# Two waits and three evictions in the preparation of a recurrent layer's chunks

## The chip, the cores and the metric

The kernel runs on one core of one Trainium2 chip. The metric is the device time of one execution in microseconds (us). A core has five engines with a queue each, which run beside one another and wait for one another by semaphores: PE (TensorE: matmuls and transposes into PSUM), DVE (VectorE), ACT (ScalarE), POOL (GpSimd) and SP (SyncE, which issues most DMAs). An engine takes its instructions in the order in which the program lists them, so one that waits holds all that stand behind it on its engine.

## The reference

A recurrence over 768 steps, for 4 batches of 8 heads with a 40x40 state each, gives the tokens of a mixture of experts:

```
for t in range(768):                     # 32 states of 40 x 40
    y[t]  = r[t] @ state
    Sa    = state @ a[t]
    state = state * w[t] - outer(Sa, b[t]) + outer(v[t], k[t])
x = y as 3072 tokens of 320
for each token: e = argmax(x @ w_gate)   # one of 8 experts
    out = softmax gate * sigmoid gate * (relu(x @ w1[e]) @ w2[e])
```

## The kernel before, in words

The 768 steps are cut into 12 chunks of 64 (c = 0 to 11); the heads are treated in two halves (q = 0, 1). A chunk goes through these stages.

- **Scan** (`scan`, lines 104 to 124): w and D (that is a, k, b) are loaded; DVE forms running products P and I of the decays (line 116, 1.8 us each), rq (line 121) and I times rq (line 123). ACT's Square (line 119) writes over w with (w - 0.9) squared and sums it up; only a check of the input's range at the end reads the sum. Before the next chunk's w can be loaded, a small DVE memset (line 108) waits for that Square. The Square reads nothing but w, but since it overwrites w it can start only when both scans have read it.
- **Prep** (`prep`, from line 137): ACT squares rq into rs (line 181, a sum for the same check). Av is put together by POOL (lines 185, 184; by DVE for chunks 0 and 1) and a small ACT copy of P (line 187). From Av come Am (line 201 on ACT and 203 on POOL for chunk 2; DMAs for other late chunks) and rows of LA. DVE forms KBt (line 212). Then, for two sides with three groups each, PE multiplies KBt and Am into a PSUM tile pl (line 225), and pl is evicted: its upper half of N (line 234 on DVE for chunk 0, line 236 on ACT for every other chunk), its lower half of N (line 236, ACT), and LA (line 238, ACT). The tiles pl, and the tiles pt of the transposes behind them (line 163, copied out by ACT at line 165), share two PSUM buffers, so PE cannot write a group before ACT has evicted the one two back.
- **Inverse** (`tinv`, line 254): DVE forms the triangular inverse T from N, chunk 0 alone, chunk 1 alone, then two chunks at a time. It begins with a transpose that needs all of N (line 266 for chunks 0 and 1; line 271 for a pair) and ends with a transpose (line 330 or 336).
- **Crit** (`crit`, line 368): the recurrence proper, for c and q one after the other: PE applies LA, T and N (lines 379 and 392), ACT moves the results (As, line 383; XU, lines 422 and 423), and for chunks 0 and 1 DVE adds a correction in two instructions (line 405, the "As pair"). The next chunk's state is formed at lines 430 to 439.
- **Tail** (`tail`, line 444): PE and DVE form the outputs pY (lines 479 and 480) and x (line 482), and the router takes x.

Behind the twelve chunks the experts follow, on PE with little else.

The order of the instructions on each engine is made by a scheduler when the program is built, from the order of the code, the buffers that come free, and its own planned times. `issue_after(m)` adds a wait: the instructions inside are placed, and issued, behind the instruction m. `s.mark['n', c]` is the last eviction of N at line 236 for chunk c, as the code has it (the last lower half of the second side). The scheduler's choices at one place change what it finds free at the next, so a small edit can move many instructions.

Of the kernel before, what the change touches and what calls it, by code (L numbers as in the profile page):

```python
# [14 lines left out]
AF = mybir.ActivationFunctionType  # L15
# [34 lines left out]
def pat(x, off, dims):  # L50

    return bass.AP(x.tensor, x.offset + off, [x.ap[0]] + [list(d) for d in dims])


class Att:
# [47 lines left out]
    def scan(s, c):  # L103

        nc, V = s.nc, s.nc.vector
        n = 12 * 2 * 33
        w = s.p1.tile([120, n + 1], F32, name="w")
        V.memset(w[:, n:], 0.0)
        nc.sync.dma_start(out=w[:, 0:n], in_=s.win[c])
        s.D = s.p1.tile([120, 12, 3, C], F32, name="D")  # L110
        s.mark[c] = nc.sync.dma_start(out=s.D, in_=s.din[c]).ins
        P, I = (s.p1.tile([120, 12, 2, 33], F32, name=x) for x in "PI")
        Pf, If = (x.rearrange("p r h t -> p (r h t)") for x in (P, I))
        with s.tc.issue_after(s.mark['t', 0]) if c == 2 else ExitStack():
            for o, d in ((Pf, w[:, 0:n]), (If[:, ::-1], w[:, n:0:-1])):
                V.tensor_tensor_scan(out=o, data0=d, data1=s.rst, initial=0.0, op0=ALU.mult, op1=ALU.add)
        wq = pat(w, 1, [(33, 24), (1, 32)])
        with s.tc.issue_after(s.mark['n', 0]) if c == 1 else ExitStack():
            nc.scalar.activation(out=wq, in_=wq, func=AF.Square, bias=s.wb, accum_out=s.wsq[:, c:c + 1])
        rq = s.p1.tile([120, 24], F32, name="rq", bufs=2)  # L120
        V.reciprocal(out=rq, in_=P[:, :, :, 32])
        I3 = I.rearrange("p r h t -> p (r h) t")
        V.tensor_tensor(out=I3, in0=I3, in1=rq.unsqueeze(2).broadcast_to([120, 24, 33]), op=ALU.mult)
        s.Q = P, I, rq
# [12 lines left out]
    def prep(s, c):  # L137

        nc = s.nc
        g, V = nc.gpsimd, nc.vector  # L140
        st = s.st[c] = {}
        P, I, rq = s.Q
# [35 lines left out]
                nc.sync.dma_start(out=LA[0:40, :, 6 * j:6 * j + ng, :], in_=Ag[40 * j:40 * j + 40, :, 0:ng])  # L178

        rs = s.p1.tile([120, 24], F32, name="rs", bufs=2)  # L180
        nc.scalar.activation(out=rs, in_=rq, func=AF.Square, accum_out=s.rqm[:, c:c + 1])
        a, kb = D[:, :, 0], D[:, :, 1:3]
        with s.tc.issue_after(s.mark['r', 0]) if c == 1 else ExitStack():
            (g if c > 1 else V).tensor_tensor(out=Av[:, :, 0:33], in0=a[:, :, 0:33], in1=I[:, :, 1, ::-1], op=ALU.mult)
            (g if c > 1 else V).tensor_tensor(out=Av[:, :, 33:64], in0=a[:, :, 33:64], in1=P[:, :, 0, 1:32], op=ALU.mult)
        with s.tc.issue_after(s.mark['n', 0]) if c == 1 else ExitStack():
            nc.scalar.copy(out=Av[:, :, 64:66], in_=P[:, :, :, 32])
        Ag = Av.rearrange("p (a g) t -> p a g t", a=2)
        if c and c != 2:
            for j in range(3):  # L190
                r, n = slice(40 * j, 40 * j + 40), 6 if j < 2 else 4
# [26 lines left out]
        for side in range(2):  # L218
            Am = s.Am[:, side]
            yield  # L220
            for g0 in range(0, 6, 2):
                pl = s.ps.tile([128, 2, 3, C], F32, name="pl", tag="pl" if c or g0 == 0 else "tl", bufs=2 if c or g0 == 0 else 3)
                nj = 3 if g0 < 4 else 2
                for i in range(2):
                    nc.tensor.matmul(pl[:, i, 0:nj], KBt[:, 6 * side + g0 + i].rearrange("p n t -> p (n t)"), Am[:, g0 + i:g0 + i + 6 * nj - 5:6, 0:64],  # L225
                                     start=True, stop=True)
                pv = pl.rearrange("p g j t -> p j g t")
                for h in range(2):
                    r = slice(64 * side + 32 * h, 64 * side + 32 * h + 32)
                    n = C - 32 * h  # L230
                    nn = pat(N[r], C * g0, [(6 * C, nj), (C, 2), (1, n)])
                    pn = pv[64 + 32 * h:96 + 32 * h, 0:nj, :, C - n:]
                    if c == 0 and not h:
                        V.tensor_scalar(out=nn, in0=pn, scalar1=-1.0, scalar2=None, op0=ALU.mult)
                    else:
                        s.mark['n', c] = nc.scalar.activation(out=nn, in_=pn, func=AF.Copy, scale=-1.0).ins  # L236
                la = pat(LA[64:128, side], 66 * g0, [(396, nj), (66, 2), (1, 64)])
                nc.scalar.activation(out=la, in_=pv[0:64, 0:nj], func=AF.Copy, scale=-1.0)  # L238
                for i in range(2):
                    g.affine_select(out=la[:, :, i], in_=la[:, :, i], pattern=[[0, nj], [1, C]], base=0, channel_multiplier=-1,  # L240
                                    compare_op=ALU.is_gt, fill=0.0)
                yield
# [344 lines left out]
class Moe:  # L587
# [346 lines left out]
    def experts(s, ctx, verdict):  # L934
# [21 lines left out]
        def unit(e, t0, nt, prep):  # L956

            for _ in s.expert(nt, W[e], T[e, t0], lambda: s.hp, ps1, ps2) if (e, t0) != (0, 0) else s.E0:
                next(prep, None)
            for _ in prep:  # L960
                pass
# [199 lines left out]
```

## Time and profile before

| what | value |
|---|---|
| time, median of 3 runs | 682.52 us (681.66 to 682.61) |
| the profiled execution's own time | 678.98 us |
| its span, first to last instruction | 677.2 us |
| PE busy | 630.9 us (93%) |
| DVE busy | 464.9 us (69%) |
| ACT busy | 340.2 us (50%) |
| POOL busy | 233.8 us (35%) |
| mean granted TensorE clock | 0.97 of full |

The profiled execution is the one that the rows below describe. Its span is 1.8 us shorter than its own time, and that time is 3.5 us under the median of the timed runs; a difference worked out in the profile is carried over to the median. A granted clock of 1.00 is 2.4 GHz and one of 0.50 is 1.2 GHz. Busy shares are means over the stretches of a program that has very different ones: the chunks run until about 440 us, the experts after that.

### The profile page before, as it was taken

How to read it: one execution, taken by the hardware profiler on the slowest of the kernel's cores; microseconds unless marked ns; L12 is line 12 of the kernel's file. 1: busy time of each engine (PE TensorE's matmuls, PEld its weight loads, DVE VectorE, ACT ScalarE, POOL GpSimd, SP SyncE). 2: the span in 40 equal slices, each digit the busy share in tenths (PEclk: the TensorE clock that was granted, in tenths of full speed). 3: DMA queues.
4: the chain of work that ended last, by engine and by line, in shares of the span. 5: the costliest groups of instructions: out<-in, count | busy, mean ns of one | idle time of the engine just before them, and what ended most of it. 6: DMA issues, size and time to landing. Idle time of an engine off the chain costs nothing. (4 is left out here: it accounts for less than half of the span.)

```text
span 677.2 us, 21154 instructions
## 1 busy us (share of the span) xinstructions
PE 630.9 (93%) x8871; PEld 564.3 (83%) x8871; DVE 464.9 (69%) x911; ACT 340.2 (50%) x783; POOL 233.8 (35%) x337
## 2 busy tenths in 40 slices
PE   7787988898999999989999889899999999999996
PEld 6475877787988888878889779799999999999985
DVE  8868689969986997699399654374774545654231
ACT  2577762784378357637743354253573435343120
POOL 9655321341144258314204111335342333211112
PEclk9667999999999999999999979999999999999999
DMA  5995763276346726643224752263774344431001
GB/s 141 179 184 132 175 156 82 78 165 168 98 128 166 157 80 168 173 97 99 83 80 126 194 165 76 58 195 85 213 203 152 115 135 134 150 103 34 19 11 32
DMA packets 56305, 84.45 MB, mean 125 GB/s; under 512 B 26848, under 2 KB 43515, under 8 KB 54763
## 3 DMA queue, kind: packets, MB, share of 16 engines
q1 hardware_dynamic: 52331, 74.05, 42.3%
q0 software_dynamic: 3872, 8.97, 4.7%
q8 instruction: 72, 1.18, 0.7%
q14 instruction: 30, 0.25, 0.1%
HBM read 67.59 MB, written 8.96 MB: 113 GB/s over the span
## 5 line engine op out<-in xcount | busy, mean ns | idle before, releaser
L863 DVE SCALAR_TENSOR_TENSOR hl<-ph,hh 128x480 fp32r<-128x480 f32 (+1 forms) x74 | 41.3, 567 | 65.4 <-ACT hh L862 65.3
L862 ACT ACTIVATE hh<-ph 128x480 fp32r<-128x480 f32 (+1 forms) x74 | 36.7, 501 | 93.5 <-PE ph L858 93.1
L878 POOL DMA_INDIRECT out_dram<-y,ti x32 | 34.3, 1073 | 141.5 <-DVE y L877 80.8
L873 PE MATMUL po<-w2h,hh 128*120 128x320 f32 x256 | 78.3, 311 | 0.2 <-ACT hh L862 0.2
L874 PE MATMUL po<-w2l,hh 128*120 128x320 f32 x256 | 77.6, 309 | 0.0
L858 PE MATMUL ph<-xh,w1h 128*128 128x480 f32 (+1 forms) x222 | 76.1, 347 | 0.3 <-DVE mem L704 0.3
L858 PE MATMUL ph<-xl,w1h 128*128 128x480 f32 (+1 forms) x222 | 75.7, 344 | 0.0
L875 PE MATMUL po<-w2h,hl 128*120 128x320 f32 x256 | 74.9, 308 | 0.0
L225 PE MATMUL pl<-Am,KBt 120*128 120x192 f32 (+1 forms) x288 | 62.9, 352 | 7.7 <-ACT LA L238 6.2
L240 POOL TENSOR_SCALAR_AFFINE_SELECT LA<-LA 64x192 f32<-64x192 f32 x144 | 55.2, 418 | 40.2 <-ACT LA L238 38.8
L383 ACT ACTIVATE As<-pa,hq 128x320 f32<-128x320 f32 x80 | 42.1, 528 | 47.2 <-PE pa L392 36.0
L236 ACT ACTIVATE N<-pl 32x192 f32<-32x192 f32 (+1 forms) x138 | 51.6, 374 | 26.3 <-PE pa L392 12.2
L225 PEld LDWEIGHTS pl<-Am,KBt 120*128 120x128 f32 x288 | 47.1, 205 | 13.4 <-ACT LA L238 8.7
L480 PE MATMUL pY<-KB,M 128*64 128x64 f32 (+1 forms) x768 | 53.3, 225 | 3.0 <-DVE M L468 3.0
L479 PE MATMUL pY<-Sd,R 128*64 128x64 f32 (+1 forms) x704 | 53.9, 227 | 0.0
L392 PE MATMUL pa<-As,Tc 64*32 64x40 f32 x1792 | 51.1, 204 | 2.9 <-ACT As L383 2.1
L730 POOL DMA_INDIRECT tab<-rec,si x24 | 29.9, 1245 | 67.6 <-DMA tab<-rec,si 45.5
L464 PE MATMUL pM<-R,VU 128*128 128x128 f32 x384 | 52.3, 287 | 0.9 <-ACT VU L456 0.8
L480 PEld LDWEIGHTS pY<-KB,M 128*64 128x64 f32 x768 | 46.9, 138 | 6.6 <-DVE M L468 3.4
L838 POOL DMA_INDIRECT xg<-xd,ti x32 | 35.8, 1118 | 44.6 <-PE px L821 32.7
L392 PEld LDWEIGHTS pa<-As,Tc 64*32 64x32 f32 x1792 | 40.3, 112 | 12.8 <-issue 3.8
L858 PE MATMUL ph<-xh,w1l 128*128 128x480 f32 (+1 forms) x148 | 50.7, 344 | 0.0
(198 smaller groups left out, 1571.2 us busy)
## 6 DMA issues: line engine op xcount, KB each, us to landing
D<-in_din_dram SPq DMA_DIRECT2D x12, 1080.0 KB
st<-in_w_dram SPq DMA_DIRECT2D x16, 512.0 KB
st<-in_w_dram SPq DMA_DIRECT2D x16, 480.0 KB
XS<-in_vt_dram SPq DMA_DIRECT2D x24, 256.0 KB
XU<-in_vt_dram SPq DMA_DIRECT2D x24, 256.0 KB
VU<-in_vl_dram SPq DMA_DIRECT2D x24, 208.0 KB
w<-in_win_dram SPq DMA_DIRECT2D x12, 371.2 KB
st<-in_w_dram SPq DMA_DIRECT2D x16, 256.0 KB
```

The source lines that it names most:

```text
L225: nc.tensor.matmul(pl[:, i, 0:nj], KBt[:, 6 * side + g0 + i].rearrange("p n t -> p (n t)"), Am[:, g0 + i:g0 + i + 6 * nj - 5:6, 0:64], sta ...
L236: s.mark['n', c] = nc.scalar.activation(out=nn, in_=pn, func=AF.Copy, scale=-1.0).ins
L240: g.affine_select(out=la[:, :, i], in_=la[:, :, i], pattern=[[0, nj], [1, C]], base=0, channel_multiplier=-1, compare_op=ALU.is_gt, fill=0.0)
L383: s.mark['as'] = nc.scalar.activation(out=x, in_=pa, func=AF.Copy, scale=s.hq[:, h:h + 1]).ins
L392: nc.tensor.matmul(pa[o + w:o + w + 32, i], m(p)[o:o + 64], x[o:o + 64, i, :], start=start, stop=True, tile_position=(o, o + w), skip_grou ...
L464: nc.tensor.matmul(pM[:, i], VU[:, h0 + i].rearrange("p n t -> p (n t)"), R[:, :, h0 + i], start=True, stop=True)
L479: nc.tensor.matmul(o, R[:, side, i, :], Sf[:, 40 * i:40 * i + w], start=True, stop=False)
L480: s.mark['y'] = nc.tensor.matmul(o, Ms[i // 4][:, i % 4, side, :], Kf[:, k:k + w], start=not c, stop=True).ins
L858: nc.tensor.matmul(ph, l, r, start=(i == 0), stop=(i == 7))
L873: nc.tensor.matmul(po, hh[f][:, ts_], w2h[:, f], start=(f == 0), stop=False)
L874: nc.tensor.matmul(po, hh[f][:, ts_], w2l[:, f], start=False, stop=False)
L875: nc.tensor.matmul(po, hl[f][:, ts_], w2h[:, f], start=False, stop=(f == 7))
```

## The change

Three edits, all in the first chunks:

1. The Square of chunk 3 is held behind the last eviction of N of chunk 2 (that of chunk 1 was already held behind chunk 0's; that of chunk 2 stays free).
2. rs of chunk 2 is held behind the last eviction of N of chunk 1.
3. The upper halves of N of chunk 1's second side (three groups) are evicted by DVE at line 234 in place of ACT at line 236.

```
@@ scan
-        with s.tc.issue_after(s.mark['n', 0]) if c == 1 else ExitStack():
+        with s.tc.issue_after(s.mark['n', c - 1]) if c in (1, 3) else ExitStack():
             nc.scalar.activation(out=wq, in_=wq, func=AF.Square, bias=s.wb, accum_out=s.wsq[:, c:c + 1])
@@ prep
         rs = s.p1.tile([120, 24], F32, name="rs", bufs=2)
-        nc.scalar.activation(out=rs, in_=rq, func=AF.Square, accum_out=s.rqm[:, c:c + 1])
+        with s.tc.issue_after(s.mark['n', c - 1]) if c in (2,) else ExitStack():
+            nc.scalar.activation(out=rs, in_=rq, func=AF.Square, accum_out=s.rqm[:, c:c + 1])
...
-        with s.tc.issue_after(s.mark['n', 0]) if c == 1 else ExitStack():
+        with s.tc.issue_after(s.mark['n', c - 1]) if c in (1,) else ExitStack():
             nc.scalar.copy(out=Av[:, :, 64:66], in_=P[:, :, :, 32])
...
-                    if c == 0 and not h:
+                    if not h and (c == 0 or c == 1 and side >= 1):
                         V.tensor_scalar(out=nn, in0=pn, scalar1=-1.0, scalar2=None, op0=ALU.mult)
                     else:
                         s.mark['n', c] = nc.scalar.activation(out=nn, in_=pn, func=AF.Copy, scale=-1.0).ins
```

The third hunk of the diff writes the wait of the small copy into Av in another form and leaves it as it was. In the kernel after, lines from 182 on stand one line lower than before (236 is 237, and so on).

The two queues below are those on which the steps of the prediction rest. The first place is ACT at the second side of chunk 1. pl_440, pl_448 and pl_456 are the three groups of that side, N_225 is N of chunks 0 and 1, w_497 belongs to chunk 2, Am_127 and Av_567 are those of chunk 2. Before:

```order
L238 ACTIVATE LA_392<-pl_440 64x3x2x64
L119 ACTIVATE w_497,wsq_142<-w_497,wb_140 120x24x32
L383 ACTIVATE As_603<-pa_541,hq_138 128x320
L181 ACTIVATE rs_569,rqm_143<-rq_507 120x24
L236 ACTIVATE N_225<-pl_448 32x3x128
L236 ACTIVATE N_225<-pl_448 32x3x2x32
L238 ACTIVATE LA_392<-pl_448 64x3x2x64
L236 ACTIVATE N_225<-pl_456 32x2x128
L236 ACTIVATE N_225<-pl_456 32x2x2x32
L238 ACTIVATE LA_392<-pl_456 64x2x2x64
L201 ACTIVATE Am_127<-Av_567,hj_134 120x2x6x64
```

And after:

```order
L119 ACTIVATE w_497,wsq_142<-w_497,wb_140 120x24x32
L384 ACTIVATE As_603<-pa_541,hq_138 128x320
L237 ACTIVATE N_225<-pl_440 32x3x2x32
L239 ACTIVATE LA_392<-pl_440 64x3x2x64
L237 ACTIVATE N_225<-pl_448 32x3x2x32
L239 ACTIVATE LA_392<-pl_448 64x3x2x64
L202 ACTIVATE Am_127<-Av_567,hj_134 120x2x6x64
L165 COPY KB_394<-pt_467 128x3x160
L237 ACTIVATE N_225<-pl_456 32x2x2x32
L239 ACTIVATE LA_392<-pl_456 64x2x2x64
L182 ACTIVATE rs_569,rqm_143<-rq_507 120x24
```

The three upper halves are gone, rs stands behind the last group, and Am of chunk 2 and a copy of KB have come ahead of that group.

The second place is ACT at the first side of chunk 2 (pl_605, pl_613; w_742, Av_761, P_747 and rs_763 belong to chunk 3). Before:

```order
L238 ACTIVATE LA_560<-pl_605 64x3x2x64
L119 ACTIVATE w_742,wsq_142<-w_742,wb_140 120x24x32
L187 COPY Av_761<-P_747 120x12x2
L181 ACTIVATE rs_763,rqm_143<-rq_752 120x24
L236 ACTIVATE N_564<-pl_613 32x3x128
L236 ACTIVATE N_564<-pl_613 32x3x2x32
L238 ACTIVATE LA_560<-pl_613 64x3x2x64
```

And after:

```order
L239 ACTIVATE LA_560<-pl_605 64x3x2x64
L188 COPY Av_761<-P_747 120x12x2
L237 ACTIVATE N_564<-pl_613 32x3x128
L237 ACTIVATE N_564<-pl_613 32x3x2x32
L239 ACTIVATE LA_560<-pl_613 64x3x2x64
L182 ACTIVATE rs_763,rqm_143<-rq_752 120x24
```

The Square has left this place (it stands 23 rows further down, behind the last group of chunk 2); the copy of P_747 still stands ahead of the second group.

The third place is DVE ahead of the inverse of chunks 2 and 3 (line 271, after: 272; I_971, P_970 and w_965 are chunk 4's; x_1087 is chunk 0's first output; As_1127 is a correction of chunk 0's second half). Before:

```order
L116 SCALAR_TENSOR_TENSOR I_971<-w_965,rst_128 120x792
L468 TENSOR_TENSOR M_1043<-pM_1038,mM_123 128x512
L116 SCALAR_TENSOR_TENSOR P_970<-w_965,rst_128 120x792
L121 RECIPROCAL rq_975<-P_970 120x24
L123 TENSOR_TENSOR I_971<-I_971,rq_975 120x792
L108 MEMSET w_1495 120x1
L482 TENSOR_TENSOR x_1087<-pY_1070,WT_224 128x320
L271 STREAM_TRANSPOSE Ns_978<-N_564 128x32x32
L276 TENSOR_TENSOR tmpf_979<-Tt_131,Ns_978 128x4
L405 TENSOR_TENSOR As_1127<-As_1127,pa_935 32x320 x2
```

And after:

```order
L483 TENSOR_TENSOR x_1087<-pY_1070,WT_224 128x320
L116 SCALAR_TENSOR_TENSOR I_971<-w_965,rst_128 120x792
L116 SCALAR_TENSOR_TENSOR P_970<-w_965,rst_128 120x792
L121 RECIPROCAL rq_975<-P_970 120x24
L123 TENSOR_TENSOR I_971<-I_971,rq_975 120x792
L108 MEMSET w_1495 120x1
L406 TENSOR_TENSOR As_1127<-As_1127,pa_935 32x320 x2
L272 STREAM_TRANSPOSE Ns_978<-N_564 128x32x32
L277 TENSOR_TENSOR tmpf_979<-Tt_131,Ns_978 128x4
```

The output x has come ahead of the two scans of chunk 4, and the As pair ahead of the inverse. From some 150 rows on, ACT has the same sequence as before but for neighbours that change places, and so has DVE.

## Rows read from the trace of the kernel before

**Rows 1.** Windows: stretch, length, then busy us (instructions) of PE, PEld, DVE, ACT, POOL, PEclk, DMA share, GB/s

```profile
60.00:66.60 6.60, 5.44 (x63) 4.38 (x64) 5.38 (x13) 5.70 (x15) 3.73 (x8) 0.50 0.22 64
66.60:87.00 20.40, 20.10 (x317) 16.77 (x317) 10.81 (x16) 15.79 (x41) 7.41 (x16) 1.00 0.64 164
87.00:132.00 45.00, 37.32 (x832) 32.11 (x830) 43.60 (x88) 22.99 (x58) 10.94 (x22) 1.00 0.42 105
```

**Rows 2.** Timeline of ACT, 58 to 60 us: start, duration, instruction, [idle before, releaser]

```profile
58.41 0.94 ACT L119 ACTIVATE w<-w,wb 120x768 f32<-120x768 f32 x1 [2.41 <-DVE P L116]
...
59.35 0.21 ACT L187 COPY Av<-P 120x24 f32<-120x24 f32 x1
...
59.79 0.82 ACT L236 ACTIVATE N<-pl 32x384 f32<-32x384 f32 x2
```

**Rows 3.** Timeline of PE, 61 us: the groups of chunk 2's second side

```profile
61.16 1.65 PE L225 MATMUL pl<-Am,KBt 120*128 120x192 f32 x4 [4.40 <-ACT LA L238]
```

**Rows 4.** Timeline of DVE, the inverse of chunks 2 and 3 and what precedes it

```profile
81.24 0.48 DVE L482 TENSOR_TENSOR x<-pY,WT 128x320 f32<-128x320 f32 x1
...
87.17 1.98 DVE L271 STREAM_TRANSPOSE Ns<-N 128x1024 f32<-128x1024 f32 x1 [5.45 <-ACT N L236]
...
89.38 0.99 DVE L405 TENSOR_TENSOR As<-As,pa 32x320 f32<-32x320 f32 x2
```

**Rows 5.** Groups by shape: N's upper halves and KB on ACT, 36 to 70 us

```profile
L236 ACT ACTIVATE N<-pl 32x384 f32<-32x384 f32 x8 | 3.9, 483 | 2.8 <-PE pl L225 2.6
...
L165 ACT COPY KB<-pt 128x480 f32<-128x480 f32 x3 | 1.7, 552 | 0.1
...
L236 ACT ACTIVATE N<-pl 32x256 f32<-32x256 f32 x4 | 1.5, 376 | 0.1
```

**Rows 6.** Groups by shape: N's upper halves on DVE (chunk 0), 15 to 30 us

```profile
L234 DVE TENSOR_SCALAR N<-pl 32x384 f32<-32x384 f32 x4 | 2.1, 549 | 0.1
...
L234 DVE TENSOR_SCALAR N<-pl 32x256 f32<-32x256 f32 x2 | 0.8, 415 | 0.4 <-PE pl L225 0.4
```

**Rows 7.** Timeline of DVE, 45 to 59 us: before the inverse of chunk 1, and chunk 3's second scan

```profile
45.30 0.06 DVE L108 MEMSET w<- 120x1 f32 x1 [3.57 <-ACT w L119]
...
47.92 1.11 DVE L266 STREAM_TRANSPOSE tmpf<-N 128x512 f32<-128x512 f32 x1
...
56.58 1.79 DVE L116 TENSOR_TENSOR_SCAN P<-w,rst 120x792 f32<-120x792 f32 x1
```

**Rows 8.** Lines of DVE, 53.3 to 56.5 us: busy us, mean ns

```profile
L276 DVE TENSOR_TENSOR tmpf<-Tt,Ns 128x32 f32<-128x32 f32 (+2 forms) x3 | 0.9, 305 | 0.1
L278 DVE TENSOR_REDUCE Tt<-tmpf 128x8 f32<-128x32 f32 (+2 forms) x3 | 0.6, 199 | 0.1
```

**Rows 9.** Timeline of POOL: Av of chunk 2

```profile
45.13 0.92 POOL L185 TENSOR_TENSOR Av<-D,P 120x372 f32<-120x372 f32 x1 [1.27 <-DMA R<-in_rl_dram]
46.12 1.16 POOL L240 TENSOR_SCALAR_AFFINE_SELECT LA<-LA 64x128 f32<-64x128 f32 x4
47.37 0.97 POOL L184 TENSOR_TENSOR Av<-D,I 120x396 f32<-120x396 f32 x1
```

**Rows 10.** Timeline of ACT: Am of chunk 2, and the Square of chunk 4

```profile
48.37 0.94 ACT L201 ACTIVATE Am<-Av,hj 120x768 f32<-120x768 f32 x1
...
79.99 0.94 ACT L119 ACTIVATE w<-w,wb 120x768 f32<-120x768 f32 x1 [0.30 <-DVE P L116]
```

**Rows 11.** Timeline of PE: chunk 3's first products, and the end of chunk 0's pY

```profile
76.08 1.57 PE L225 MATMUL pl<-Am,KBt 120*128 120x192 f32 x8
...
80.19 0.26 PE L480 MATMUL pY<-KB,M 128*64 128x40 f32 x2
```

**Rows 12.** Where the next pair of chunks picks up: ACT, chunk 4

```profile
122.16 0.82 ACT L236 ACTIVATE N<-pl 32x384 f32<-32x384 f32 x2 [4.81 <-PE pa L392]
```

**Rows 13.** Timeline of PE: a late gap

```profile
391.81 1.29 PE L430 MATMUL pS<-XU,KB 128*40 128x40 f32 x16 [2.50 <-DVE tmS L434]
```

**Rows 14.** Windows, columns as in rows 1: the clock behind that gap

```profile
392.00:394.00 2.00, 2.00 (x20) 1.92 (x20) 1.94 (x3) 1.37 (x3) 1.70 (x2) 0.50 0.34 99
```

More of the change, by code (lines that the diff above doesn't have):

```diff
@@ L117, in scan @@
         wq = pat(w, 1, [(33, 24), (1, 32)])
-        with s.tc.issue_after(s.mark['n', 0]) if c == 1 else ExitStack():
+        with s.tc.issue_after(s.mark['n', c - 1]) if c in (1, 3) else ExitStack():
             nc.scalar.activation(out=wq, in_=wq, func=AF.Square, bias=s.wb, accum_out=s.wsq[:, c:c + 1])
@@ L180, in prep @@
         rs = s.p1.tile([120, 24], F32, name="rs", bufs=2)
-        nc.scalar.activation(out=rs, in_=rq, func=AF.Square, accum_out=s.rqm[:, c:c + 1])
+        with s.tc.issue_after(s.mark['n', c - 1]) if c in (2,) else ExitStack():
+            nc.scalar.activation(out=rs, in_=rq, func=AF.Square, accum_out=s.rqm[:, c:c + 1])
         a, kb = D[:, :, 0], D[:, :, 1:3]
@@ L185, in prep @@
             (g if c > 1 else V).tensor_tensor(out=Av[:, :, 33:64], in0=a[:, :, 33:64], in1=P[:, :, 0, 1:32], op=ALU.mult)
-        with s.tc.issue_after(s.mark['n', 0]) if c == 1 else ExitStack():
+        with s.tc.issue_after(s.mark['n', c - 1]) if c in (1,) else ExitStack():
             nc.scalar.copy(out=Av[:, :, 64:66], in_=P[:, :, :, 32])
@@ L232, in prep @@
                     pn = pv[64 + 32 * h:96 + 32 * h, 0:nj, :, C - n:]
-                    if c == 0 and not h:
+                    if not h and (c == 0 or c == 1 and side >= 1):
                         V.tensor_scalar(out=nn, in0=pn, scalar1=-1.0, scalar2=None, op0=ALU.mult)
```

## The prediction

> **What bounds the kernel now.** I read the windows first, since the change lies in the first eighth of the span. Between 60 and 66.6 us the granted clock is 0.50, from 66.6 us on it is 1.00; from 66.6 to 87 PE is busy for 20.10 of 20.40 us, and from 87 to 132 DVE is busy for 43.60 of 45.00 us [rows 1]. So PE, which makes N of chunk 3, has no idle time ahead of 87 us, and DVE none behind it. What ties the two is seen in DVE's timeline: the inverse of chunks 2 and 3 starts at 87.17 after DVE has been idle for 5.45 us, released by an eviction of N on ACT [rows 4]. What matters is when chunk 3's last N arrives, and how much DVE does between that and its next idle time.
>
> Next I read, at the place of the change, who waits for whom. ACT stands idle for 2.41 us until DVE's scan P of chunk 3 ends and the Square may start at 58.41; the Av copy and the second group of chunk 2 follow, that group at 59.79 [rows 2]. PE needs the buffer which that group frees and idles for 4.40 us before 61.16 [rows 3]. That gap is followed by the half clock.
>
> **The change part by part.** All times are of the profiled execution (678.98 us, with 1.8 us outside its span); the difference is then laid on the median.
>
> *The evictions handed to DVE.* ACT is rid of two of 483 ns and one of 376 ns [rows 5], 1.34 us. DVE takes two of 549 and one of 415 [rows 6], 1.51 us. They come where DVE idled for 3.57 us before 45.30 [rows 7], so DVE's end pays nothing as long as the tiles pl arrive as before; if that cover went, 1.51 us would be paid.
>
> *What moved at that place.* Am of chunk 2 now stands on ACT ahead of chunk 1's last group (first place of the change). Am reads Av, of which POOL made the parts at 45.13 and 47.37, with LA work between [rows 9]; before, Am ran at 48.37, behind all of N [rows 10]. In the new order one half of the 1.16 us of LA work still precedes POOL's second part: 45.13 + 0.92 + 0.58 + 0.97 = 47.6. Then come Am (0.94, [rows 10]), a KB copy (0.55, [rows 5]) and the last lower half, for which I allow 0.3, estimated under the 376 ns of the larger upper half [rows 5]: 49.4. Chunk 1's inverse, which began at 47.92 [rows 7], waits for it: +1.5 us. Bounds: 0 (POOL is early) to +2.4 (POOL at its old time, 47.37 + 0.97 = 48.34, plus Am, KB and the half, ends 50.1, and 0.2 for waits). Chunk 1's inverse is not what the pair of chunks 2 and 3 waits for, so I take nothing for it at 87 us.
>
> *The Square of chunk 3.* It leaves ACT at 58.41 and runs behind chunk 2's last group instead, at about 68, inside the stretch in which ACT is one of the engines that feed PE. But the small copy of P stays ahead of the second group (second place), and it reads the same scan P. That scan ended at 56.58 + 1.79 = 58.37 [rows 7]. In the new order the inverse of chunk 1 starts 1.5 later; six of its small steps, 3 x 305 + 3 x 199 ns = 1.5 us [rows 8], fall behind the scan; an As pair of 0.99 [rows 4] comes ahead of it. So the scan ends at 58.37 + 1.5 - 1.5 + 0.99 = 59.4, bounds 58.37 (all of it in idle time) and 60.9 (no small step spared). The copy of 0.21 [rows 2] follows, and the group starts at 59.6 where it was at 59.79. The stall of ACT therefore changes hands and gains 0.2 us; the Square's 0.94 is paid later. With the half clock kept, I take 0 for the arrival of chunk 3's N, the value nearest to the row of the wait [rows 2]. Lower end: the inverse at 87.17 cannot start earlier than by DVE's idle 5.45 [rows 4]. Upper end: the 4.5 us of the second rival.
>
> The trace says PE is full from 66.6 to 87 by its busy time (20.10 of 20.40), but its weight loads only fill 16.77 [rows 1]. The Trainium skill ("Trainium Kernel Development and Optimization", section Performance Expectations) calls matmul busy time a bad metric, because matmuls are pipelined, and the share of LDWEIGHTS a good one. By busy time each us won before 66.6 would arrive at 87 in full, and by the skill's measure 18% of that stretch is slack that could swallow it; no run here yet decides it.
>
> *rs of chunk 2.* It moves from inside chunk 1's groups to behind them. One ACT row of its kind, the small copy of P, takes 0.21 us [rows 2]; the stretch gains that, and it is within my allowances: 0.
>
> *The third place, on DVE.* The As pair (0.99 us, at 89.38, behind the first step of the inverse) now stands ahead of the inverse, in the idle 5.45 us [rows 4]. From 87 on DVE has 1.40 us of idle time in 45 [rows 1], so the inverse ends 0.99 earlier. Where it ends, the next chunks take over: ACT begins N of chunk 4 at 122.16, after waiting 4.81 us for PE's pa [rows 12], which comes out of the crit chain fed by this inverse. All later sequences are the same, so the shift is passed on. Bounds: 0 (lost in the 1.40 us of slack) and -0.99; I take -0.99. Cover gone (pa of that pair late by over 5.45): it would cost its own lateness.
>
> Sum: 0 (evictions) + 0 (inverse of chunk 1) + 0 (Square) + 0 (rs) - 0.99 (third place) = **-1.0 us**: 678.0 us for the profiled execution, and 682.52 - 1.0 = **681.5 us** for the median.
>
> **The rivals.**
>
> *The gain is real.* If the scan ends at its lower bound and the second group starts early enough that PE's gap of 4.40 us [rows 3] does not pull the clock down, the 6.60 us at 0.50 [rows 1] run at full speed: 3.3 us come back, and with the 0.99 it is -4.3: 678.2 us. For it: PE is full behind it. Against it: the copy waits for the very scan the Square waited for, so the gap remains, and weight loads leave slack.
>
> *Slower: x ahead of the scans.* At the third place the output x of chunk 0 has come ahead of the two scans of chunk 4. x needs pY, whose last product ended at 80.19 + 0.26 = 80.45 [rows 11]. In the new order of PE all of pY stands ahead of chunk 3's first products (76.08 before, [rows 11]), so pY should end by about 76. If it does not, and ends at 80.45, the scans follow x: 80.45 + 0.48 [rows 4] + 2 x 1.79 [rows 7] = 84.5, and the Square of chunk 4, at 79.99 before [rows 10], which waits for them and has four groups of chunk 3's N behind it on ACT, is 4.5 late. That makes 4.5 - 0.99 = +3.5: 686.0 us. It breaks even where pY ends at 80.45 - 3.5 = 77.0, and is slower by over 0.2% (1.36 us) from 78.3 on.
>
> *The clock falls earlier.* The wait for Am leaves PE without a buffer until chunk 1's last group is out at 49.4, a gap of about 1.8 us (Am 0.94, the copy 0.55, the half 0.3). After a gap of 2.50 us late in the kernel [rows 13] the clock was 0.50 for at least 2 us of full work [rows 14]. Half speed for 2 us costs 1.0 us, and the wait of 4.40 [rows 3] behind it would absorb more than that at first. It cancels the 0.99: 682.5 us.
>
> The Trainium skill ("TensorE: Matmul & The Clock Gate", section Part 1) has throttled as the default state, which activity releases. The rows agree so far: both gaps are followed by 0.50. By that rule this rival's full price would be that of the first gap, 3.3 us, not 1.0, and the time 684.8.
>
> *The shift is lost.* The As pair's 0.99 us ends in slack, and the change does nothing but hand the stall from the Square to the copy: 682.5 us.
>
> **How the numbers follow.** Forecast 0.45, the real gain 0.22, x ahead of the scans 0.20, the earlier clock and the lost shift together 0.13. A measurement of this kernel can tell about 0.2%, 1.36 us, from no change: 681.16 to 683.88. The forecast lies inside by 0.3 us only, with 1.6 us of spread from the bounds of the scan and of chunk 1's inverse, so 0.18 of its 0.45 is faster, 0.23 the same and 0.04 slower. With the real gain, faster is 0.40. The same is 0.23 + 0.13 = 0.36. x ahead gives slower, 0.20 + 0.04 = 0.24. The likeliest case alone has the range 679.9 to 683.1; to hold 8 in 10 the range takes in most of the real gain and most of the way to 686.0: 678.0 to 685.6.
>
> **What would show it.** In the trace after: ACT idles ahead of the Av copy, not of the Square, and the copy runs near 59.4 (else the hand-over is wrong); the clock from 60 to 66.6 is 0.50 (1.00 would be the first rival); chunk 1's inverse starts near 49.4, after ACT's wait for Av; pY ends before 77 and the scans of chunk 4 start by then (later is the second rival); the inverse of the pair starts near 87.2 with the As pair in front of it; N of chunk 4 starts 1.0 earlier than 122.16. If the inverse starts well off 87.2 in either direction the main term is wrong.

## The result, and the profile after

The changed kernel takes 688.84 us (median of 5, 686.52 to 689.44) against 682.52: a ratio of 1.0093 with an interval of 1.0076 to 1.0110, slower by 6.3 us where 681.5 was forecast. The profiled execution after took 689.44 us (span 687.6); the one before was 3.5 us below its median, so the two traces lie further apart (10.4 us of span) than the times do. Here and below a time is the median of all executions, while a ratio is that of the means without the slow executions (over 1.5% above the fastest of their kernel), so the two need not match.

Windows of the kernel after (PE, PEld, DVE, ACT, POOL busy, PEclk, DMA share, GB/s), which answer to [rows 1]:

```profile
60.00:66.60 6.60, 6.09 (x95) 4.88 (x89) 6.36 (x16) 5.32 (x16) 5.25 (x9) 0.87 0.14 29
66.60:87.00 20.40, 18.26 (x209) 15.27 (x209) 11.40 (x20) 9.39 (x23) 1.60 (x6) 0.67 0.55 146
87.00:132.00 45.00, 37.32 (x810) 32.22 (x810) 38.26 (x80) 21.59 (x56) 10.39 (x19) 0.96 0.41 100
```

From 66.6 to 87 PE gets through 209 matmuls where it did 317, at a granted clock of 0.67 where it was 1.00; from 87 on DVE has idle time again (38.26 of 45.00 us busy, where it was 43.60). The clock is 0.50 from 72 to 85 us. One stretch of that, before and then after (same columns):

```profile
75.00:80.00 5.00, 5.00 (x89) 4.28 (x90) 4.89 (x6) 2.87 (x8) 1.58 (x1) 1.00 0.96 210
```

```profile
75.00:80.00 5.00, 5.00 (x58) 4.20 (x58) 3.00 (x4) 1.00 (x3) 0.00 (x0) 0.50 0.44 118
```

Timeline of ACT after, which answers to [rows 2]:

```profile
61.08 0.23 ACT L188 COPY Av<-P 120x24 f32<-120x24 f32 x1 [1.26 <-issue]
61.33 0.82 ACT L237 ACTIVATE N<-pl 32x384 f32<-32x384 f32 x2
```

The second group of chunk 2 starts 1.5 us later than before, not 0.2 earlier. Timeline of PE after, from pM to chunk 3's first products ([rows 11]):

```profile
72.68 3.78 PE L465 MATMUL pM<-R,VU 128*128 128x128 f32 x16 [0.56 <-ACT VU L457]
...
82.16 1.51 PE L481 MATMUL pY<-KB,M 128*64 128x64 f32 x24
...
84.54 2.08 PE L226 MATMUL pl<-Am,KBt 120*128 120x192 f32 x8
```

Those products begin at 84.54 where they began at 76.08, behind all of pY. Timeline of DVE after, up to the inverse of chunks 2 and 3 ([rows 4]):

```profile
83.72 0.49 DVE L483 TENSOR_TENSOR x<-pY,WT 128x320 f32<-128x320 f32 x1 [3.72 <-PE pY L481]
...
94.80 0.99 DVE L406 TENSOR_TENSOR As<-As,pa 32x320 f32<-32x320 f32 x2 [4.56 <-PE pa L393]
95.87 1.99 DVE L272 STREAM_TRANSPOSE Ns<-N 128x1024 f32<-128x1024 f32 x1
```

The inverse starts at 95.87, 8.7 us later than before. Timelines of ACT, the last eviction of chunk 3's N, before and then after:

```profile
86.48 0.66 ACT L236 ACTIVATE N<-pl 32x256 f32<-32x256 f32 x2
```

```profile
95.19 0.65 ACT L237 ACTIVATE N<-pl 32x256 f32<-32x256 f32 x2
```

N is complete at 95.84 (87.14 before), and in both kernels the inverse starts 0.03 us behind it. The As pair, which waits for PE's pa, ends at 95.79, just ahead of N. So what comes 8.7 us late is N; the pair in front of the inverse is hidden behind it. The delay is there at chunk 3's first group already (its eviction starts at 86.00, before at 77.03); from there to the last N both kernels take about 10 us.

### The profile page after: what moved, and what is told of

Read it like the earlier page. It is cut to its first block, busy times and chain, and to the rows that moved or that the text cites. A ratio compares the mean times of both kernels' runs of the same rounds, so it can differ in the third digit from the quotient of the medians.

```text
span 687.6 us, 21158 instructions
## 1 busy us (share of the span) xinstructions
PE 636.5 (93%) x8871; PEld 568.3 (83%) x8871; DVE 466.8 (68%) x914; ACT 337.8 (49%) x780; POOL 227.1 (33%) x337
## 5 line engine op out<-in xcount | busy, mean ns | idle before, releaser
L241 POOL TENSOR_SCALAR_AFFINE_SELECT LA<-LA 64x192 f32<-64x192 f32 x144 | 52.9, 400 | 51.6 <-ACT LA L239 50.2
L237 ACT ACTIVATE N<-pl 32x192 f32<-32x192 f32 (+1 forms) x135 | 50.1, 371 | 32.3 <-PE pa L393 15.7
L481 PE MATMUL pY<-KB,M 128*64 128x64 f32 (+1 forms) x768 | 55.0, 231 | 3.9 <-DVE M L469 3.9
L481 PEld LDWEIGHTS pY<-KB,M 128*64 128x64 f32 x768 | 48.4, 143 | 7.5 <-DVE M L469 4.3
L731 POOL DMA_INDIRECT tab<-rec,si x24 | 28.5, 1189 | 68.4 <-DMA tab<-rec,si 37.7
```

The source lines that it names most:

```text
L481: s.mark['y'] = nc.tensor.matmul(o, Ms[i // 4][:, i % 4, side, :], Kf[:, k:k + w], start=not c, stop=True).ins
```

## The experiments

All ratios are to runs of the kernel before on the same chip.

**Each edit alone, and one wait put back.** The first three take one hunk of the diff each; x_am adds to the changed kernel

```
+                    with s.tc.issue_after(s.mark['n', 1]) if c == 2 else ExitStack():
                         e.activation(out=o, in_=i, func=AF.Copy, scale=m)      # Am
```

- e1_square. 

> The kernel before with the first edit alone: the Square of chunk 3 behind the last N of chunk 2. Theory O (the time was lost because the third edit, the evictions on DVE, led the scheduler to put PE's pM ahead of chunk 2's last transposes and all of pY ahead of chunk 3's first products): here pM stays behind the transposes, so the inverse of chunks 2 and 3 starts within 2 us of 87.2 and the time is 680 to 684 us. Theory S (the held Square, 0.94 us on ACT ahead of VU and KB copies, delays PE and starts the half clock): the inverse starts 4 us late or more and the time is 686 to 689 us.


- e2_rs. 

> The kernel before with the second edit alone: rs of chunk 2 behind the last N of chunk 1; two rows of ACT change places. Every theory: within 1.4 us of 682.5.


- e3_evict. 

> The kernel before with the third edit alone: three upper halves of N of chunk 1 on DVE; the Square of chunk 3 is as before. Theory O: the order of PE is that of the changed kernel, the inverse of chunks 2 and 3 starts 5 us late or more (92 or later) and the time is 686 to 690 us. Theory S: without the held Square nothing is lost, 681 to 684 us.


- x_am. 

> The changed kernel with one wait added: Am of chunk 2 on ACT is held behind chunk 1's last N, where it stood before, so that ACT does not wait for POOL ahead of that N. In this program chunk 3's first products stand behind half of pY only, but pM still ahead of two of chunk 2's transposes. Theory C (the loss starts with ACT's wait for Am: chunk 1's inverse late by 1.7 us, a gap of PE, the half clock from 50 to 60): the clock from 50 to 60 is 1.00, chunk 1's inverse starts by 48, and at least half of the 6.3 us comes back, 685.5 us or less. Theory O in its strict form (only the place of pY counts): about half, 685 to 686. Theory S: the loss stays, 688 to 689 us, since the Square is still held.

Measured: e1_square 693.04 us (1.0160, 1.0087 to 1.0234); e2_rs 681.46 (0.9979, 0.9948 to 1.0011); e3_evict 688.88 (1.0083, 1.0047 to 1.0119); x_am 691.33 (1.0100, 1.0020 to 1.0181). The third edit alone gives the whole loss, with the inverse at 95.19; rs is nothing. Theory C is not borne out: in x_am chunk 1's inverse starts at 48.58, the clock from 50 to 60 is 0.66, and nothing comes back. But its loss lies elsewhere: its inverse of chunks 2 and 3 starts at 91.66, the one two later at 213.04 (212.44 before), and the last one at 345.16 (337.69). The first edit alone is slow too, and neither theory had that: its inverse of chunks 2 and 3 is in time, the loss comes later. Timeline of DVE of e1_square, that inverse and the one two later (212.44 in the kernel before):

```profile
88.20 1.97 DVE L271 STREAM_TRANSPOSE Ns<-N 128x1024 f32<-128x1024 f32 x1 [5.56 <-ACT N L236]
...
217.36 1.97 DVE L271 STREAM_TRANSPOSE Ns<-N 128x1024 f32<-128x1024 f32 x1
```

In e1_square, e3_evict and x_am the scheduler has moved rows far behind the edit too, so these runs can't tell an edit from an order.

**Order or edits.** Therefore the order of each engine was written out, as a chain of issue-order edges at the end of the recurrence, over instructions that have the same names in all versions:

```
+        for a, b in zip(names, names[1:]):      # names: one engine's order, as another program has it
+            tc.add_manual_dep(traced[b], a, NoSync)
```

- o_old. 

> All three edits, but the order of every engine's instructions is written out as that of the kernel before: only the three evictions go from ACT to DVE, rs stands behind chunk 1's last N, and the Square of chunk 3 (with the DMA and the memset of w that wait for it) behind chunk 2's last LA. Theory O (the loss is the order into which the scheduler brings all engines, not the three edits): the inverse of chunks 2 and 3 starts within 1.5 us of 87.2 and the time is 680 to 684 us. Theory E (the edits themselves cost it: evictions on DVE are slower, the Square is in the way later): the inverse starts 4 us late or more, 686 to 690 us.


- o_new. 

> The mirror: none of the three edits, but the order of every engine's instructions is written out as that of the changed kernel; the three upper halves of N of chunk 1 are back on ACT, each just ahead of its lower half. Theory O: the loss is there without the edits; the inverse of chunks 2 and 3 starts at 94 to 98 and the time is 687 to 691 us. Theory E: 681 to 684 us.


- o_old_evict. 

> The third edit alone in the written-out order of the kernel before: only three evictions change their engine. Theory O: chunk 1's inverse starts within 0.5 us of 47.9, the time is within 1.4 us of 682.4. Theory E: 685 us or more, as the run of the third edit alone had 688.9.


- o_old_stall. 

> No edit; the written-out order of the kernel before, with three rows of ACT moved: the Square of chunk 3, the small copy of P and rs of chunk 3 stand behind the third group of chunk 2 in place of ahead of the second, so that the second group waits for no scan. If ACT's stall of 2.41 us and PE's gap of 4.40 us are what the order before pays (the first rival of the prediction): the second group starts at 56 to 57 where it was at 59.79, the granted clock from 60 to 66.6 is above 0.8, the inverse of chunks 2 and 3 starts 2 to 4.5 us earlier and the time is 678 to 681 us. If the stall is hidden by what chunk 3 waits for otherwise (its scan, Am's DMAs): 682 to 683 us.

The rows that o_old_stall moves on ACT:

```
-L119 w_742 (Square)   -L187 Av_761<-P_747   -L181 rs_763
 L236 N_564<-pl_613 ... L238 LA_560<-pl_613   L383 As_952   L236 N_564<-pl_621 ... L238 LA_560<-pl_621
+L119 w_742 (Square)   +L187 Av_761<-P_747   +L181 rs_763
```

Measured: o_old 681.54 us (0.9987, 0.9963 to 1.0012), o_new 688.73 (1.0110, 1.0076 to 1.0143). All three edits in the old order are as fast as before; the new order without any edit has the whole loss. So the cause is the order. o_old_evict is 680.67 (0.9974, 0.9949 to 1.0000), a little under the 681.0 to 683.8 expected. Timelines of DVE, the inverse of chunks 2 and 3, of o_old and then of o_new (this one short of the 94 expected):

```profile
87.56 1.97 DVE L272 STREAM_TRANSPOSE Ns<-N 128x1024 f32<-128x1024 f32 x1 [5.43 <-ACT N L237]
```

```profile
91.44 0.99 DVE L405 TENSOR_TENSOR As<-As,pa 32x320 f32<-32x320 f32 x2 [4.57 <-PE pa L392]
92.52 1.99 DVE L271 STREAM_TRANSPOSE Ns<-N 128x1024 f32<-128x1024 f32 x1
```

In o_new, too, N ends last: it is complete at 92.49, the pair at 92.43.

o_old_stall is 682.59 (1.0008, 0.9982 to 1.0034): taking ACT's stall away is worth nothing here. Its timelines of ACT and of PE:

```profile
56.95 0.82 ACT L236 ACTIVATE N<-pl 32x384 f32<-32x384 f32 x2
```

```profile
62.88 1.28 PE L392 MATMUL pa<-As,Tc 64*32 64x40 f32 x34 [3.64 <-DVE As L405]
```

The second group starts 2.8 us earlier than in [rows 2], but PE's gap of 4.40 us [rows 3] is now one of 3.64: the crit rows ahead of the next products wait for DVE's As. The clock from 60 to 66.6 is 0.74 (above 0.8 expected), and the inverse of chunks 2 and 3 starts at 88.02, not earlier. So a new wait has taken the old one's place; what the stretch is worth without any gap on PE, this run doesn't show.

**Single places undone in the new order.**

```
n_am   ACT:  -L202 Am_127  -L165 KB_394<-pt_467   L237 N_225<-pl_456  L239 LA_392<-pl_456   +L202 Am_127  +L165 KB_394
n_pe   PE:   +pt_704 +pt_710   pM x8   +pt_714 +pt_738   pa_935<-Tc   +pl_797 +pl_823   pY x16 ...    DVE: KBt_792 ahead of M
```

n_am_pe is both; n_pe_x is n_pe with x_1087 behind chunk 4's scans on DVE.

- n_am. 

> The changed kernel in its own written-out order, but for two rows of ACT: Am of chunk 2 and the KB copy stand behind the last group of chunk 1 again. Theory A (the loss begins there: chunk 1's inverse late, its Tc copies late on ACT ahead of chunk 2's last group, and all that follows): chunk 1's inverse starts by 48.7, the inverse of chunks 2 and 3 starts 2 us earlier or more than the changed kernel's 92.5 to 95.9, and the time is 685 to 687 us. Theory P (only the place of pM and pY on PE, ahead of chunk 2's last transposes and chunk 3's first products, counts): chunk 1's inverse is earlier, but the pair's is not by more than 1 us, 688 to 689 us.


- n_pe. 

> The changed kernel in its own written-out order, but for PE and one place on DVE: chunk 2's last transposes stand ahead of pM, chunk 3's first two groups of products ahead of pY, KBt of chunk 3 ahead of the two M. Theory P: the first group of chunk 3 is evicted by 82 where the changed kernel had 86.0, the inverse of the pair starts by 91 and the time is 684 to 686 us. Theory A: the late start stays, the pair's inverse gains 1.5 us at most, 687 to 689 us.


- n_am_pe. 

> Both moves together. If A and P each carry a part, the parts add up: the inverse of the pair starts at 87 to 90 and the time is 682 to 685 us. If it stays above 686, the loss sits in a place that neither names.


- n_pe_x. 

> The run in which PE's rows of chunk 3 were moved forward in the order of the changed kernel, and in addition the output x of chunk 0 on DVE moved behind chunk 4's two scans, where the kernel before has it. In that run the third group of chunk 3 stood behind the Square of chunk 4 at 87.50, which waited for the scans, and these for x. Theory X (the second rival of the prediction, x ahead of the scans, is what kept that run late): the Square of chunk 4 runs by 83, the inverse of the pair starts by 91 and the time is 685 to 688 us. If x does not matter: 690 us or more.

Measured: n_am 687.42 us (1.0097, 1.0061 to 1.0133), n_pe 693.73 (1.0141, 1.0084 to 1.0198), n_am_pe 691.90 (1.0160, 1.0125 to 1.0194), n_pe_x 692.77 (1.0142, 1.0103 to 1.0180). None brings it back, and with n_am_pe above 686 the loss sits in a place that neither theory names. In n_am chunk 1's inverse starts at 48.57, but ends as late as in the changed kernel, and theory A falls. In n_pe the eviction of chunk 3's first group starts at 81.78, about as expected, and the next wait is the one priced as the second rival, the Square behind the scans behind x. Timelines of ACT and of DVE of n_pe:

```profile
81.78 0.82 ACT L237 ACTIVATE N<-pl 32x384 f32<-32x384 f32 x2
83.12 0.82 ACT L237 ACTIVATE N<-pl 32x384 f32<-32x384 f32 x2
87.50 0.94 ACT L119 ACTIVATE w<-w,wb 120x768 f32<-120x768 f32 x1 [2.52 <-DVE P L116]
```

```profile
93.21 0.99 DVE L406 TENSOR_TENSOR As<-As,pa 32x320 f32<-32x320 f32 x2 [4.38 <-PE pa L393]
94.28 1.99 DVE L272 STREAM_TRANSPOSE Ns<-N 128x1024 f32<-128x1024 f32 x1
```

Here too N (complete at 94.26) ends just behind the pair. With x moved back (n_pe_x) the Square waited for no scan but still ran at 86.66, not by 83, and the As pair waited 7.40 us, to 95.78. It ended at 96.77, 0.2 us behind N, so in this run the pair is the last wait. The time stays at 690 or more, and theory X falls as well.

**The order cut into stretches**, with the third edit alone:

```
h_new_old:   new order to chunk 2's last N,  then old
h_old_new:   old order to chunk 2's last N,  then new
h_old_late:  old order to chunk 3's last N,  then new
```

- h_new_old. 

> The third edit alone, the order written out: up to chunk 2's last N (about 70 us) that of the changed kernel, behind it that of the kernel before. Theory E1 (the early stretch makes the loss: chunk 1's second side, its back transposes, chunk 2's products behind the crit rows of chunk 0): 686 to 689 us, chunk 2's last N at 69.5 to 70.5. Theory M (the middle stretch from there to the inverse of chunks 2 and 3 makes it): 682 to 684 us.


- h_old_new. 

> The same the other way round: up to chunk 2's last N the order of the kernel before, behind it that of the changed kernel. Theory M: 686 to 689 us, the inverse of chunks 2 and 3 starts at 91 or later although chunk 2's last N is evicted by 68.5. Theory E1: 682 to 684 us, the inverse starts by 89.


- h_old_late. 

> The third edit alone; up to chunk 3's last N (the start of the inverse of chunks 2 and 3) the order of the kernel before, behind it that of the changed kernel. Theories E1 and M: the loss lies ahead of that point, 680 to 683.5 us. Theory L (the later order is worse by itself, as in the run of the first edit alone, where the inverse of the pair was in time and the loss came behind 192 us): 685 us or more.

Measured: 687.63 us (1.0076, 1.0045 to 1.0107), 689.46 (1.0078, 1.0046 to 1.0110), 686.93 (1.0078, 1.0052 to 1.0105). E1, M and L each find the loss in the run of their own stretch, but E1 and M deny it to the others (h_old_new lies a little over its 686 to 689, with the inverse at 90.37 where 91 or later was expected): every stretch costs nearly as much as all, and the costs don't add up. They meet at one event, the start of the inverse. Timelines of DVE, h_new_old and then h_old_new:

```profile
91.34 1.99 DVE L271 STREAM_TRANSPOSE Ns<-N 128x1024 f32<-128x1024 f32 x1 [5.45 <-ACT N L236]
```

```profile
89.30 0.99 DVE L405 TENSOR_TENSOR As<-As,pa 32x320 f32<-32x320 f32 x2 [4.56 <-PE pa L392]
90.37 1.99 DVE L271 STREAM_TRANSPOSE Ns<-N 128x1024 f32<-128x1024 f32 x1
```

With the early stretch new, N is 4.2 us late (complete at 91.31), and the pair stands behind it. In h_old_new N is 3.2 us late (complete at 90.34), and the pair ends just ahead of it, as in the changed kernel. With only the stretch behind chunk 3's N new, N is in time and the pair is late. Timelines of h_old_late, ACT's last group of chunk 3 and then DVE:

```profile
87.85 0.66 ACT L236 ACTIVATE N<-pl 32x256 f32<-32x256 f32 x2
```

```profile
90.38 0.99 DVE L405 TENSOR_TENSOR As<-As,pa 32x320 f32<-32x320 f32 x2 [7.29 <-PE pa L392]
91.40 1.97 DVE L271 STREAM_TRANSPOSE Ns<-N 128x1024 f32<-128x1024 f32 x1
```

N is complete at 88.5; the inverse starts at 91.40, because the As pair stands ahead of it.

**That pair alone, and what the same wait is worth the other way.**

```
o_old_as   DVE:  +L405 As_1127 x2   L271 Ns_978<-N_564   L276 tmpf_979   -L405 As_1127 x2     (in the order of o_old_evict)
o_best2    DVE:  -L405 As_1127 x2   L278, L276 (13 steps of the inverse)   +L405 As_1127 x2   (in the order of o_best)
```

- o_old_as. 

> The third edit alone in the written-out order of the kernel before, with one thing of the changed kernel's order: on DVE the As pair of chunk 0's second half stands ahead of the inverse of chunks 2 and 3 instead of behind its first step (the third place of the change, which the prediction counted as a gain of 0.99 us). Theory W (the pair waits for its pa, which PE delivers at about 89 in the trace of before, and holds the inverse): DVE waits some 7 us ahead of the pair, the inverse starts at 90 to 91.5 where this order has it at 87.2 to 88.2, and the time is 684 to 686.5 us against 680.7 for this order without the move. As the prediction had it: the inverse starts no later, 679.5 to 681 us.


- o_best. 

> The third edit in the written-out order of the kernel before, with rows moved so that chunk 3's N comes sooner: the Square, the copy of P and rs of chunk 3 behind chunk 2's third group; the fifth group ahead of XU and Tc; the four KB copies of chunk 2 ahead of As; KBt of chunk 3 two rows earlier on DVE; Am's DMAs ahead of LA's; chunk 3's products and evictions ahead of pY, of the Square of chunk 4 and of three crit copies. If chunk 3's N is what the pair's inverse waits for (5.45 us in the rows of before): the inverse starts at 82.5 to 85 and the time is 677 to 680 us. If the crit chain of chunk 0's second half, moved behind, takes its place: the shift is lost by 131.9, where the inverse ends, and the time is 681 to 684 us.


- o_best2. 

> The order in which chunk 3's N comes 6 us sooner, with one more move on DVE: thirteen small steps of the inverse go ahead of the As pair, for which DVE had waited 3.54 us at 83.7. If that wait is what took most of the gain: the wait falls under 1.5 us, the inverse ends at 125 to 127.5 (129.0 without the move, 131.9 in the kernel before) and the time is 676 to 679 us. If the crit chain sets the pace from there on: 679 to 681 us.

Measured: o_old_as 684.52 us (1.0061, 1.0022 to 1.0100; o_old_evict, without the move, 0.9949 to 1.0000). Theory W holds; its timeline of DVE:

```profile
89.17 0.99 DVE L405 TENSOR_TENSOR As<-As,pa 32x320 f32<-32x320 f32 x2 [7.37 <-PE pa L392]
90.19 1.97 DVE L271 STREAM_TRANSPOSE Ns<-N 128x1024 f32<-128x1024 f32 x1
```

N is complete at 87.22 here; the inverse starts 3.0 us later. Behind it PE waits too, and the clock is 0.50 from 94 to 104 us, where o_old_evict has 1.00; how much of the time that makes up is not shown.

o_best has the inverse at 81.43, but DVE then waits 3.54 us for the pair behind the first step, and the time is 679.54 (0.9981, 0.9952 to 1.0010): no clear gain. With steps of the inverse put ahead of the pair, o_best2 takes **676.26 us (0.9948, 0.9917 to 0.9979)** and beats both kernels. Timeline of DVE of o_best2:

```profile
80.80 2.00 DVE L271 STREAM_TRANSPOSE Ns<-N 128x1024 f32<-128x1024 f32 x1
...
87.23 0.36 DVE L278 TENSOR_REDUCE Tt<-tmpf 128x28 f32<-128x196 f32 x1
87.60 0.99 DVE L405 TENSOR_TENSOR As<-As,pa 32x320 f32<-32x320 f32 x2
...
128.53 2.14 DVE L336 STREAM_TRANSPOSE Tc<-Tt 128x1024 f32<-128x1024 f32 x1
```

The wait ahead of the pair is gone. The end of the inverse (128.53 against 131.92 before) came short of the 125 to 127.5 expected; where the other half of the 6.4 us of its earlier start goes was not followed.

## Why the prediction was wrong, step by step

- **The Square and the arrival of chunk 3's N (0): the step that failed.** The prediction followed the stall at chunk 2's second group and, with the half clock kept, took 0 for the arrival of N. N was complete at 95.84 in place of 87.14: +8.7 us, and the inverse started right behind it. The new order of PE, all of pY ahead of chunk 3's products, was used for one consequence alone, that pY ends by 76. It ended at 83.67 (82.16 + 1.51), and the products that now stood behind it began 8.5 us late. The price of what a moved row is moved ahead of was left out. That this comes with the order and not with the edits, o_old (0.9987) and o_new (1.0110) show; h_new_old, with the pair in its old place, shows that a late N alone costs the time (1.0076).
- **The third place, on DVE (-0.99 us): wrong too, but hidden in the changed kernel.** It put the As pair into DVE's idle 5.45 us as if the pair were ready. Its pa was not. In the trace of before PE delivers it only here (timeline of PE, 88 us):

```profile
88.22 0.76 PE L392 MATMUL pa<-As,Nm 64*32 64x40 f32 x32 [0.27 <-ACT As L383]
```

  That ends at 88.98, 7.3 us after DVE fell idle and behind the inverse's start at 87.17: the prediction named this case (cover gone) and didn't look it up. Ahead of an inverse whose N is in time the pair must wait, and the inverse with it: 88.98 + 0.99 - 87.17 = 2.8 us later, not 0.99 won. o_old_as shows the wait (7.37 us), and its ratio of 1.0061, where the order without the move has 0.9974. In the changed kernel N came so late that the pair cost the start nothing; from start to end the inverse took 44.6 us (95.87 to 140.44) for 44.8 (87.17 to 131.92), 0.2 won.
- **The shift passed on: right, for a wrong reason.** ACT's row at 122.16 [rows 12] lies ahead of the inverse's last step (131.92), so this inverse can't feed it. The next inverse did move with it: 159.26 for 149.58, +9.7.
- **Chunk 1's inverse (+1.5, harmless): size right, "harmless" not shown.** It began at 49.63 (49.4 predicted) after ACT's wait for Am, and its end at 69.11 releases ACT's Tc copies ahead of chunk 2's last group, whose N is complete at 70.72 (68.48 before). But undoing that wait alone (n_am) changes neither that end nor the time clearly.
- **Evictions on DVE (0) and rs (0): right as costs of their own.** In the old order the evictions cost nothing (o_old_evict), and rs alone costs nothing (e2_rs). But the evictions alone bring a new order and the whole loss (e3_evict).
- **Hand-over of the stall from the Square to the copy: right in kind.** The copy ran at 61.08 instead of 59.4, right behind the scan (ended at 61.00), ACT idle 1.26 us ahead of it. The clock from 60 to 66.6 was 0.87, not 0.50.
- **First rival, a real gain: not borne out.** In o_old_stall, without ACT's stall, PE has a gap of 3.64 us in place of the 4.40, and nothing is won.
- **Second rival, x ahead of the scans: on the right side, for another reason.** pY ended late and x waited 3.72 us, as this rival has it. But in the changed kernel the Square of chunk 4, at 89.11, waited for no scan: the scans had ended at 87.62, and ACT had been held up to 86.00 by chunk 3's products. n_pe shows the rival's wait, and n_pe_x that it was not the one that decided.
- **Third rival, the clock: seen, in part separated.** The clock was 0.62 from 50 to 56 us and 0.67 from 66.6 to 87. From 46 to 92 us it was 0.92 in the profile of before, 0.93 in h_old_new, 0.85 in h_new_old and in o_new, and 0.74 in the changed kernel; chunk 3's N came 3.2, 4.2, 5.4 and 8.7 us late in the last four. So the new order behind chunk 2's last N makes N late at the clock of before as well (h_old_new). How much of the 8.7 us is the lower clock no run shows; each figure is from one execution.

Still open: which rows of the new order make chunk 2's and 3's N late, how much of that is the clock, and why the first edit alone loses its time between the inverse at 149.41 and the one at 217.36.

## What to carry to other kernels

When a scheduler reorders, price the order before the edit. Find the row on which the time hangs (here the start of the inverse) and take the new order of the engine that runs it and of the engines that feed it (here PE and ACT). For each row that has come ahead, add its time, and look up when its input was ready before: if that is later than the input of the critical row, the critical row now waits for it. Undoing one place proves little when several late inputs meet at one instruction; the one that the profile names as released last can be ahead of another by 0.05 us, so look up the end of each. Writing out the old order with the edits, and the new order without them, decides in two runs whether an edit or its reordering costs the time.

## What was not expected of the hardware

Executions differ by more than was taken for a measurement's reach: 12 runs of o_old span 678.36 to 685.52 us. Two programs with nearly the same order of rows (the edits alone set them apart) started the same inverse at 92.52 in one profile (o_new) and at 95.87 in another (the changed kernel). The granted clock from 50 to 60 us was 1.00 in the first and 0.62 (to 56) and 0.50 (from 56) in the second.
